# Two weight pieces split on TensorE and ScalarE, and the first layer of two chunks in two halves: one fused attention and MLP kernel with every step in a new order

## The chip, the cores and the metric

The kernel runs on one core of one Trainium2 chip. Its time is the device time of one execution in microseconds (us). Three runs of the kernel before gave 561.91 to 562.13, median 562.1.

## The reference

Inputs are q, k and v of 4 batches, 8 heads, 768 positions and 64 columns, and the weights w_in (512 x 2048) and w_out (2048 x 512), which arrive as 64-bit floats. Cut to what matters:

```
k_sum = k.reshape(B, H, nb, 32, D).max(axis=3)       # one summary key per block of 32
v_sum = v.reshape(B, H, nb, 32, D).mean(axis=3)
scores_l = where(|i - j| < 16, scale * q @ k.T, -1e9)   # a band around the diagonal
scores_s = scale * q @ k_sum.T + log(32)
a = exp(s - max(s));  a = a / (sum(a) + 1e-9)         # s: band and summaries side by side
x = a @ concat(v, v_sum)                               # heads put together: 3072 x 512
h = x @ w_in
out = 0.5 * h * (1 + erf(h / sqrt(2))) @ w_out
```

## The kernel before

The attention is cut into 24 **units**, each one batch, four heads and 256 queries. Two units give the 512 columns of 256 tokens, a **chunk**; there are 12. In a unit of the first batches the steps are: `f_mask`/`f_scores` or `scores` (products on TensorE), `evac` or `add_mask`, `maximum` (an all-reduce over partitions on GpSimd), `m_shift` (TensorE) or `shift` (VectorE), `exponent` (ScalarE), `f_sums`/`sums` and `f_values`/`values` (TensorE), then `norm_take`, `norm_rec`, `norm_spread`, `norm_mult` on VectorE with `norm_cross` on ScalarE between the first two, and last `x_hi` (ScalarE) and `x_lo` (VectorE), which leave the unit's output as a high and a low half in f16.

Nearly all matrix products are three f16 products in place of one f32 product: high by high, high by low, low by high. So each weight is split as well. `w_in` comes in eight **pieces** of 256 columns, one DMA of 1024 KB each (`fetch_w_in`). A piece is turned from the 64-bit pattern into f32 by three VectorE instructions (`wi_bits i 0` to `2`, L458, L463, L467), its high half is written by ScalarE (`wi_hi`, L493) and its low half by one VectorE instruction, `wi_lo` (L496: weight times 128 less the high half). `w_out` goes the same way (`wo_bits`, `wo_hi`, `wo_lo`).

The first layer of chunks 0 to 3 is `phase1 c i` (L990 to L992): 24 products of 128x256, over all four quarters of the contraction, for chunk c and piece i, into one of three PSUM tiles (`psh`). Quarters 0 and 1 come from the chunk's first unit, 2 and 3 from its second. `gelu`, `g_hi` (ScalarE) and `g_lo` (VectorE) follow, and `phase2 c n` (L1109 to L1111) is a quarter of the second layer for half of the tokens. Batches 1 to 3 later take fewer products by Strassen's rule (`sp`, `so` and the sums around them).

Three things matter for the order. All engines work through their instructions strictly in the order in which the program issues them, and a table of steps written out by hand (`ORDER`, some 1,780 steps) sets that order for all engines at once, the DMA issues on SyncE's queue (SP) included. Buffers are handed out by tables of slots (`SLOTS`), so a step also waits until the slot's last user is done. And in the first 36 us the table has steps `fill n`: each is three products of 512 columns or six of 256 of a tile of ones (L409), whose result nobody reads. Sixteen more such products are issued at the start.

Lines that the prediction touches: L409 fill, L618 `sum_vt` (f32 products for the means of v of batch 0), L690 `s_load_vs` (ScalarE copies the means into a unit's v tile), L777 `f_values`, L796 `s_q_hi`, L805 `q_lo`, L949 `norm_cross`, L952 `norm_rec`, L963 `norm_mult`, L970 `x_lo`, L443 `fetch_w_in` and `fetch_w_out`, L666 `load_q`, L675 `load_v`.

Of the kernel before, what the change touches and what calls it, by code (L numbers as in the profile page):

```python
# [79 lines left out]
load_ind, wi_bits 0 0, fetch_k 0 1, f_mask 0, f_scores 0, fetch_vt 0, fill 4, fill 11, load_q 1, evac 0, maximum 0,  # L80
k_pack 2, wi_bits 0 1, wi_bits 0 2, fetch_w_in 4 4, fill 12, sum_vt 0, wi_hi 0, s_k_hi 3, fetch_w_in 5 5, prep_k 0 1,
wi_lo 0, fill 8, k_pack 1, f_mask 1, m_shift 0, load_q 2, m_exponent 0, f_scores 1, f_mask 2, fetch_vt 1, f_sums 0,
fetch_vt 2, evac 1, prep_k_end 0 1, load_v 0, f_scores 2, k_lo 3, load_q 3, wi_bits 4 0, wi_bits 4 1, wi_bits 4 2,
wi_hi 4, wi_bits 5 0, maximum 1, norm_take 0, evac 2, wi_bits 5 1, wi_bits 5 2, norm_cross 0, sum_vt 1, sum_vt 2,
s_q_hi 3, fill 0, mean_vt, m_shift 1, norm_rec 0, s_load_vs 0, fetch_w_in 2 2, load_v 1, f_values 0, fill 3,
norm_spread 0, fetch_w_in 3 3, wi_lo 4, q_lo 3, load_v 2, wi_bits 2 0, m_exponent 1, k_sums 0 1, wi_bits 2 1,
norm_mult 0, maximum 2, s_load_vs 1, x_hi 0, f_sums 1, load_q 4, load_vs 2, m_shift 2, m_exponent 2, wi_bits 2 2,
norm_take 1, x_lo 0, wi_bits 3 0, f_values 1, wi_bits 3 1, load_k 4, f_mask 3, norm_cross 1, scores 3, evac 3,
norm_rec 1, fetch_w_in 1 1, norm_spread 1, load_v 4, wi_hi 5, wi_bits 3 2, fill 10, s_k_hi 4, f_sums 2, norm_mult 1,
x_hi 1, s_q_hi 4, norm_take 2, k_lo 4, wi_hi 3, x_lo 1, maximum 3, load_k 5, wi_lo 5, fill 2, wi_bits 1 0, f_mask 4,  # L90
norm_cross 2, f_values 2, load_v 3, phase1 0 4, fetch_k 1 3, gelu 0 4, q_lo 4, phase1 0 0, wi_bits 1 1, phase1 0 5,
shift 3, wi_hi 2, load_vs 3, wi_bits 1 2, norm_rec 2, load_vs 4, scores 4, exponent 3, norm_spread 2, wi_lo 3, wi_hi
1, g_hi 0 4, fetch_w_in 6 2, norm_mult 2, prep_k 1 3, f_sums 3, wi_lo 2, gelu 0 0, norm_take 3, load_q 5, x_hi 2,
norm_cross 3, f_values 3, wi_lo 1, wi_bits 6 0, gelu 0 5, norm_rec 3, x_lo 2, fetch_k 1 0, fetch_w_in 7 3, norm_spread
3, prep_k 1 0, evac 4, g_hi 0 5, maximum 4, norm_mult 3, phase1 0 3, s_k_hi 5, phase1 0 1, x_hi 3, fetch_w_out 0 4,
g_hi 0 0, wi_bits 6 1, phase1 0 2, s_q_hi 5, k_lo 5, gelu 0 3, fetch_w_out 1 5, x_lo 3, phase1 1 4, q_lo 5, shift 4,
exponent 4, wi_bits 6 2, load_k 6, g_lo 0 4, f_mask 5, gelu 0 1, wo_bits 0 0, s_k_hi 6, f_sums 4, g_lo 0 0, scores 5,
wo_bits 0 1, wi_bits 7 0, load_v 5, g_hi 0 3, g_lo 0 5, f_values 4, gelu 0 2, g_hi 0 1, phase1 1 1, wo_bits 0 2,
fetch_k 2 1, wi_bits 7 1, wo_hi 0, wo_bits 1 0, gelu 1 4, g_lo 0 1, wi_bits 7 2, phase1 1 3, gelu 1 1, fetch_w_out 2
4, norm_take 4, wo_bits 1 1, wo_lo 0, g_lo 0 3, wi_hi 6, wo_bits 1 2, phase1 1 5, wi_hi 7, phase1 1 0, g_hi 1 4, evac  # L100
5, g_lo 1 4, load_q 6, gelu 1 3, wi_lo 7, wo_hi 1, wi_lo 6, f_mask 6, s_q_hi 6, g_hi 0 2, q_lo 6, wo_lo 1, gelu 1 5,
fetch_k 1 1, maximum 5, g_hi 1 5, g_lo 1 5, g_hi 1 1, g_hi 1 3, phase1 1 2, norm_cross 4, phase1 0 7, prep_k 1 1,
prep_k 2 1, wo_bits 2 0, g_lo 1 3, wo_bits 2 1, norm_rec 4, phase2 0 0, wo_bits 2 2, g_lo 0 2, norm_spread 4,
load_mask, gelu 1 2, load_q 7, fetch_w_out 3 5, gelu 1 0, g_hi 1 0, wo_bits 3 0, gelu 0 7, prep_k_end 1 0, wo_bits 3
1, g_lo 1 1, wo_bits 3 2, phase1 0 6, phase1 1 7, k_sums 1 0, k_lo 6, load_vs 5, g_hi 1 2, fetch_w_out 4 4, shift 5,
s_q_hi 7, phase2 0 1, gelu 0 6, norm_mult 4, wo_hi 3, wo_hi 2, exponent 5, wo_lo 3, phase1 1 6, wo_bits 4 0,
fetch_w_out 5 5, wo_lo 2, wo_bits 4 1, scores 6, f_sums 5, evac 6, wo_bits 5 0, wo_bits 4 2, x_hi 4, wo_bits 5 1,
f_values 5, wo_hi 4, norm_take 5, norm_cross 5, wo_bits 5 2, wo_lo 4, f_mask 7, wo_hi 5, load_k 7, wo_lo 5, norm_rec
# [1343 lines left out]
```

## Time and profile before

| | |
|---|---|
| median of three runs | 562.1 us |
| profiled execution | 562.31 us |
| its span, first to last instruction | 560.5 us |
| TensorE busy | 552.6 us, 99% |
| VectorE busy | 472.6 us, 84% |
| ScalarE busy | 384.8 us, 69% |
| GpSimd busy | 94.7 us, 17% |
| DMA | 64.30 MB, mean 115 GB/s |
| granted TensorE clock | 1.000 |

The profiled execution has 1.8 us outside its span and lies 0.2 us above the median. The shares are means over the whole span. VectorE is busy without a break for the first 120 us and has idle time later, and the DMA engines are full from 9 to 30 us only, so what an edit in the first part is worth has to be read from that part.

### The profile page before, as it was taken

What the parts mean: (1) busy time and instruction counts of PE and PEld (TensorE: products, weight loads), DVE (VectorE), ACT (ScalarE), POOL (GpSimd) and SP (SyncE); (2) the same over time, 40 slices, a digit from 0 to 9 for tenths busy, and PEclk for the clock granted to TensorE, in tenths of its full rate; (3) what the DMA queues carried; (4) which work ended last, traced back from release to release, by engine and by line L of the source; (5) the groups of instructions that cost most, each with busy time, mean ns of one, the idle gap of its engine ahead of it and who ended that gap; (6) DMA issues with size and microseconds to landing.
All of it is one profiled execution on the core that took longest, in us unless ns stands there. A gap on an engine that the chain in (4) does not pass through costs nothing.

```text
span 560.5 us, 13994 instructions
## 1 busy us (share of the span) xinstructions
PE 552.6 (99%) x6011; PEld 402.2 (72%) x6011; DVE 472.6 (84%) x660; ACT 384.8 (69%) x665; POOL 94.7 (17%) x42
## 2 busy tenths in 40 slices
...
GB/s 320 396 274 389 189 154 191 266 130 207 158 163 116 146 64 107 144 81 139 91 148 90 28 130 115 63 65 2 22 19 1 20 1 2 2 1 48 1 48 57
DMA packets 29230, 64.30 MB, mean 115 GB/s; under 512 B 2800, under 2 KB 8688, under 8 KB 29168
## 3 DMA queue, kind: packets, MB, share of 16 engines
...
q10 hardware_dynamic: 288, 0.34, 0.2%
q14 instruction: 15, 0.12, 0.1%
HBM read 55.34 MB, written 6.29 MB: 110 GB/s over the span
## 4 chain that ended last, share of the span: by engine, by line
PE 76%; DVE 17%; DMA 3%; issue 2%; ACT 1%; SPq 0%; DVEq 0%
PE psy L1061 13%; PE pso L1109 9%; PE pso L1110 9%; PE pso L1111 9%; PE psz L1061 7%; PE psd_y L1297 4%; PE pso_y L1297 3%; PE pss_x L1297 3%; PE psx L1061 3%; PE psv L913 3%; PE psh L990 2%; PE psh L991 2%; PE psh L992 2%; PE pss L831 2%; DMA w_out_h<-in_vt_dram 2%
## 5 line engine op out<-in xcount | busy, mean ns | idle before, releaser
L860 POOL PARTITION_ALL_REDUCE m<-s x23 | 82.4, 3582 | 284.4 <-DVE s L851 114.2
L1109 PE MATMUL pso<-w_out_h,gg 128*128 128x512 f16 x256 | 97.1, 379 | 0.0
L1111 PE MATMUL pso<-w_out_h,gg 128*128 128x512 f16 x256 | 97.0, 379 | 0.0
L1110 PE MATMUL pso<-w_out_l,gg 128*128 128x512 f16 x256 | 97.0, 379 | 0.0
L1061 PEld LDWEIGHTS <-wt 128*128 128x128 f16 x768 | 74.7, 98 | 12.1 <-issue 0.6
L991 PE MATMUL psh<-xos,ww 128*128 128x256 f16 x256 | 69.8, 273 | 0.8 <-DVE xos L970 0.8
L990 PE MATMUL psh<-xos,ww 128*128 128x256 f16 x256 | 69.8, 273 | 0.1
L1061 PE MATMUL psy<-xos,wt 128*128 128x256 f16 x576 | 69.8, 273 | 0.0
L992 PE MATMUL psh<-xos,ww 128*128 128x256 f16 x256 | 69.8, 273 | 0.0
L1061 PEld LDWEIGHTS <-ww 128*128 128x128 f16 x576 | 56.0, 98 | 9.8 <-issue 0.2
L1111 PEld LDWEIGHTS <-gg 128*128 128x128 f16 x256 | 25.0, 98 | 30.5 <-DVE gg L1093 0.4
L1109 PEld LDWEIGHTS <-gg 128*128 128x128 f16 x256 | 25.0, 98 | 25.9
L1110 PEld LDWEIGHTS <-gg 128*128 128x128 f16 x256 | 25.0, 98 | 25.8
L1297 PEld LDWEIGHTS <-gg 128*128 128x128 f16 x384 | 37.6, 98 | 5.1 <-issue 0.3
L1072 ACT ACTIVATE ww<-psy 128x512 f32<-128x512 f32 x48 | 27.8, 588 | 13.7 <-PE psy L1061 10.9
L1189 DVE SCALAR_TENSOR_TENSOR gg<-h,gg 128x512 f16<-128x512 f32 x32 | 21.7, 684 | 11.1 <-ACT gg L1186 11.1
L1093 DVE SCALAR_TENSOR_TENSOR gg<-g,gg 128x512 f16<-128x512 f32 x32 | 22.7, 711 | 8.0 <-ACT gg L1089 7.9
L865 DVE TENSOR_TENSOR s<-s,m 128x1024 f32<-128x1024 f32 x21 | 25.5, 1217 | 4.3 <-POOL m L860 4.3
L990 PEld LDWEIGHTS <-ww 128*128 128x128 f16 x256 | 25.0, 98 | 4.2 <-issue 0.2
L992 PEld LDWEIGHTS <-ww 128*128 128x128 f16 x256 | 25.0, 98 | 4.1 <-issue 1.2
L991 PEld LDWEIGHTS <-ww 128*128 128x128 f16 x256 | 25.0, 98 | 3.8
L999 ACT ACTIVATE g<-psh 128x512 f32<-128x512 f32 x32 | 18.9, 593 | 11.4 <-DVE gg L1008 8.7
...
## 6 DMA issues: line engine op xcount, KB each, us to landing
...
```

What stands on the lines that cost most here:

```text
L860: nc.gpsimd.partition_all_reduce(out_ap=self.m32, in_ap=self.s32, channels=P, reduce_op=bass_isa.ReduceOp.max)
L865: nc.vector.tensor_tensor(out=self.s32, in0=self.s32, in1=self.m32, op=ALU.subtract)
L990: nc.tensor.matmul(ph[:, e, :], wh, xh, start=(k == 0), stop=False)
L991: nc.tensor.matmul(ph[:, e, :], wh, xl, start=False, stop=False)
L992: nc.tensor.matmul(ph[:, e, :], wl, xh, start=False, stop=(k == NCC - 1))
L1061: nc.tensor.matmul(ps[:, e, :], ws, xx, start=(first and e == 0 and k == 0 and m == 0), stop=(k == 1 and m == 2), skip_group_check=True,)
L1072: nc.scalar.activation(snaps[b, q, n], split8(acc[b, q, "y"]), AF.Copy)
L1093: nc.vector.scalar_tensor_tensor(out=g_part(o // 2, q, 1, fs), in0=g32t.pop((b, q, o)), scalar=SC_G, in1=g_part(o // 2, q, 0, fs), op0=ALU ...
L1109: nc.tensor.matmul(p, gh, w_out_h[:, f, :], start=(f == 0), stop=False)
L1110: nc.tensor.matmul(p, gh, w_out_l[:, f, :], start=False, stop=False)
L1111: nc.tensor.matmul(p, gl, w_out_h[:, f, :], start=False, stop=(f == NFC - 1))
L1297: nc.tensor.matmul(ps, g, ww_, start=(first and e == 0 and k == 0), stop=(e == 1 and k == 2), skip_group_check=True,)
```

## The change

Pieces 0 and 4 of `w_in` get their low halves in another way. `wi_lo 0` and `wi_lo 4` go. In their place TensorE forms 128 times the weight less its high half in PSUM, in two halves of 512 columns (`wi_diff i h`: one f32 product with a scaled identity, one f16 product with a negated one), and ScalarE copies each half to its place (`wi_dlo i h`). `load_neg` makes the negated identity on ScalarE once. `phase1` of chunks 0 and 1 is replaced by `p1h c i 0` and `p1h c i 1`, twelve products each: the first needs only the chunk's first unit and quarters 0 and 1 of the weight. Seven of the nine `fill` steps go. All steps stand in a new order, and the slots follow it.

```
-PE_DIFF = 0
+PE_DIFF = 2
...
 ORDER = '''
-a_load_q 0, fill 1, fetch_k 0 0, prep_k 0 0, a_load_m16, prep_k_end 0 0, k_pack 0, fetch_w_in 0 0, k_sums 0 0,
...
+a_load_q 0, a_load_m16, fetch_k 0 0, prep_k 0 0, k_pack 0, fill 8, prep_k_end 0 0, fetch_w_in 0 0, fetch_vt 0, k_pack
...
+    def p1h(c, i, h):
+        if h == 0:
+            pht[c, i] = ps_h.tile([P, 2, CH], F32, tag="psh", name=f"psh_{c}_{i}")
+        ph, x = pht[c, i], xo[2 * c + h]
+        for e in range(2):
+            for k in range(2):
+                wh, wl = (ww[:, z, 2 * h + k, e, i, :] for z in range(2))
+                xh, xl = (x[:, z, k, :] for z in range(2))
+                for m, (ws, xx) in enumerate(((wh, xh), (wh, xl), (wl, xh))):
+                    nc.tensor.matmul(
+                        ph[:, e, :], ws, xx, start=(h == 0 and e == 0 and k == 0 and m == 0),
+                        stop=(h == 1 and k == 1 and m == 2), skip_group_check=True,
+                    )
```

The steps that are now called and were there unused before:

```
    def load_neg():
        nc.scalar.activation(neg, eye, AF.Copy, scale=-1.0 / SC_WI)
    def wi_diff(i, h):
        ps = diffs["i", i, h] = ps_h.tile([P, 2, CH], F32, tag="psh", name=f"psw_{i}_{h}")
        flat = ps.rearrange("p e j -> p (e j)")
        ks = slice(2 * h, 2 * h + 2)
        nc.tensor.matmul(flat, eye, wt[:, i, h * 512 : (h + 1) * 512], start=True, stop=False)
        nc.tensor.matmul(flat, neg, w_part(i, 0, ks), start=False, stop=True)
    def wi_dlo(i, h):
        flat = diffs.pop(("i", i, h)).rearrange("p e j -> p (e j)")
        ks = slice(2 * h, 2 * h + 2)
        nc.scalar.activation(w_part(i, 1, ks), flat.rearrange("p (r j) -> p r j", j=P), AF.Copy)
```

First place: TensorE around the first `sum_vt` (`psv_vt`). Before:

```order
L409 MATMUL pso_fill_189<-ones 64x512
L618 MATMUL psv_vt<-w_out_h,w_out_l 88x512 x2
L409 LDWEIGHTS ones
L409 MATMUL psd_fill_201<-ones 64x256
L409 LDWEIGHTS ones
L409 MATMUL psd_fill_201<-ones 64x256
```

And after, where `psw` is the PSUM tile of a `wi_diff` and the identities stand in the room of `w_out_l`:

```order
L410 MATMUL psd_fill_178<-ones 64x256
L619 MATMUL psv_vt<-w_out_h,w_out_l 88x512 x2
L505 MATMUL psw_0_196<-wt,w_out_l 128x512
L506 LDWEIGHTS w_out_l
L506 MATMUL psw_0_196<-ww,w_out_l 128x512
L505 MATMUL psw_1_200<-wt,w_out_l 128x512
L506 LDWEIGHTS w_out_l
L506 MATMUL psw_1_200<-ww,w_out_l 128x512
L732 LDWEIGHTS mask_sb
```

The fill behind `sum_vt` has become the two halves of piece 0's low half.

Second place: VectorE from the reciprocal of unit 0 (`rc`) to its `norm_mult` (`x32s<-psv`). Before:

```order
L952 RECIPROCAL rc_287<-rc_287 128x16
L956 STREAM_TRANSPOSE dent_282<-rc_287 128x512
L496 SCALAR_TENSOR_TENSOR ww<-wt,ww 128x1024
L805 TENSOR_TENSOR ql_341<-q_3_273,qh_297 128x512
L458 TENSOR_SCALAR wt<-gg 128x1024
L463 SCALAR_TENSOR_TENSOR wt<-gg,wt 128x1024
L963 TENSOR_TENSOR x32s<-psv_314,dent_282 128x512
L467 SCALAR_TENSOR_TENSOR wt<-gg,wt 128x1024
```

After:

```order
L953 RECIPROCAL rc_284<-rc_284 128x16
L957 STREAM_TRANSPOSE dent_261<-rc_284 128x512
L459 TENSOR_SCALAR wt<-gg 128x1024
L464 SCALAR_TENSOR_TENSOR wt<-gg,wt 128x1024
L468 SCALAR_TENSOR_TENSOR wt<-gg,wt 128x1024
L964 TENSOR_TENSOR x32s<-psv_308,dent_261 128x512
L806 TENSOR_TENSOR ql_343<-q_3_255,qh_326 128x512
```

The low half of piece 4 is gone, the third step of piece 2 has moved ahead of `norm_mult`, and the low half of unit 3's q has moved behind it.

Third place: DMA issues on SP from `load_q 2` on. Before, where `gg` is the raw room for pieces 2 and 3:

```order
L666 DMA q_2_219<-in_qd_dram 128x512
L612 DMA w_out_h<-in_vt_dram 128x1024 x2
L675 DMA v_0_254<-in_vw_dram 128x1024
L666 DMA q_3_273<-in_qd_dram 128x512
L443 DMA gg<-in_w_in_dram 128x4x512
L675 DMA v_1_312<-in_vw_dram 128x1024
```

After:

```order
L667 DMA q_2_185<-in_qd_dram 128x512
L613 DMA w_out_h<-in_vt_dram 128x1024 x2
L444 DMA gg<-in_w_in_dram 128x4x512
L676 DMA v_0_223<-in_vw_dram 128x1024
L667 DMA q_3_255<-in_qd_dram 128x512
L444 DMA gg<-in_w_in_dram 128x4x512
L676 DMA v_1_328<-in_vw_dram 128x1024
```

Piece 2 (1024 KB) now goes ahead of unit 0's v (512 KB) and unit 3's q (256 KB).

## Rows read from the trace of the kernel before

**Rows 1.** The page: busy time, share of the span, instructions.

```profile
PE 552.6 (99%) x6011; PEld 402.2 (72%) x6011; DVE 472.6 (84%) x660; ACT 384.8 (69%) x665; POOL 94.7 (17%) x42
```

**Rows 2.** Waits of TensorE: who, for whom; us, times, longest.

```profile
PE psn L785 <- ACT s L868: 1.0, 1, 1.0
PE pso_fill_s L409 <- POOL warm L421: 0.9, 1, 0.9
PE psh L991 <- DVE xos L970: 0.8, 2, 0.5
PE psv L777 <- issue: 0.6, 1, 0.6
```

**Rows 3.** Busy us by stretch: PE, PEld, DVE, ACT, POOL; clock, DMA, GB/s.

```profile
10.00:20.00 10.00, 9.66 (x84) 5.53 (x82) 9.86 (x11) 6.58 (x11) 3.84 (x1) 1.00 1.05 398
20.00:30.00 10.00, 9.67 (x100) 5.61 (x96) 9.76 (x11) 7.59 (x16) 7.32 (x2) 1.00 1.04 391
...
100.00:120.00 20.00, 19.54 (x150) 14.37 (x148) 19.67 (x27) 14.92 (x24) 4.19 (x1) 1.00 0.57 205
...
200.00:300.00 100.00, 100.00 (x1148) 66.90 (x1141) 92.49 (x134) 77.36 (x132) 17.99 (x6) 1.00 0.35 106
```

**Rows 4.** Waits of VectorE, 0 to 120 us: all of them.

```profile
DVE ks_f L591 <- DMA w_out_l<-in_kp_dram: 6.2, 1, 6.2
DVE wt L458 <- DMA gg<-in_w_in_dram: 0.8, 1, 0.8
```

**Rows 5.** Timeline of TensorE: start, duration, line, operation, count, [idle before].

```profile
0.94 5.61 PE L409 MATMUL pso_fill_s<-ones 128*64 128x512 f16 x16 [0.94 <-POOL warm L421]
...
10.43 0.83 PE L409 MATMUL pso_fill<-ones 128*64 128x512 f16 x3
11.10 0.82 PE L409 MATMUL psd_fill<-ones 128*64 128x256 f16 x6
...
12.91 1.92 PE L618 MATMUL psv_vt<-w_out_h,w_out_l 128*88 128x512 f32 x4 [0.34 <-DMA w_out_h<-in_vt_dram]
...
27.66 1.15 PE L777 MATMUL psv<-s,v 128*64 128x64 f32 x32
...
39.55 0.27 PE L991 MATMUL psh<-xos,ww 128*128 128x256 f16 x1 [0.37 <-DVE xos L970]
...
46.53 0.27 PE L992 MATMUL psh<-xos,ww 128*128 128x256 f16 x1
...
107.98 0.27 PE L991 MATMUL psh<-xos,ww 128*128 128x256 f16 x1 [0.46 <-DVE xos L970]
```

**Rows 6.** Timeline of VectorE, the same columns.

```profile
14.00 1.25 DVE L496 SCALAR_TENSOR_TENSOR ww<-wt,ww 128x1024 f16<-128x1024 f32 x1
...
25.21 2.00 DVE L496 SCALAR_TENSOR_TENSOR ww<-wt,ww 128x1024 f16<-128x1024 f32 x1
27.14 0.68 DVE L805 TENSOR_TENSOR ql<-q,qh 128x512 f16<-128x512 f32 x1
...
29.83 0.68 DVE L963 TENSOR_TENSOR x32s<-psv,dent 128x512 f32<-128x512 f32 x1
30.43 1.22 DVE L467 SCALAR_TENSOR_TENSOR wt<-gg,wt 128x1024 int32<-128x1024 int32 x1
...
37.53 1.36 DVE L799 TENSOR_TENSOR k_all<-k,k_all 128x640 f16<-128x640 f32 x1
...
89.53 0.82 DVE L799 TENSOR_TENSOR k_all<-k,k_all 128x640 f16<-128x640 f32 x1
...
107.23 0.69 DVE L970 TENSOR_TENSOR xos<-x32s,xos 128x512 f16<-128x512 f32 x1
```

**Rows 7.** Timeline of ScalarE, the same columns.

```profile
25.28 0.63 ACT L796 ACTIVATE qh<-q 128x512 f16<-128x512 f32 x1 [1.19 <-DMA q<-in_qd_dram]
...
26.55 1.05 ACT L690 ACTIVATE v<-w_out_h 24x1024 f32<-24x1024 f32 x1
...
41.60 0.60 ACT L999 ACTIVATE g<-psh 128x512 f32<-128x512 f32 x1
```

More of the change, by code (lines that the diff above doesn't have):

```diff
@@ L78 @@
 ORDER = '''
-a_load_q 0, fill 1, fetch_k 0 0, prep_k 0 0, a_load_m16, prep_k_end 0 0, k_pack 0, fetch_w_in 0 0, k_sums 0 0,
[L80 to L108, printed above, removed]
@@ new lines @@
+wi_dlo 0 1, load_q 3, wi_hi 4, k_sums 0 0, wi_bits 5 1, norm_take 0, wi_bits 5 2, f_mask 2, f_scores 2, evac 2,
+norm_cross 0, sum_vt 1, sum_vt 2, k_sums 0 1, norm_rec 0, norm_spread 0, maximum 2, fetch_w_in 3 3, wi_diff 4 0,
+m_shift 1, mean_vt, s_load_vs 0, f_values 0, wi_bits 2 0, s_q_hi 3, load_v 1, m_shift 2, load_v 2, wi_dlo 4 0, load_vs
+2, fetch_k 1 3, wi_bits 2 1, wi_bits 2 2, norm_mult 0, m_exponent 1, q_lo 3, wi_bits 3 0, f_sums 1, fetch_w_in 1 1,
+wi_diff 4 1, norm_take 1, x_hi 0, m_exponent 2, norm_cross 1, x_lo 0, f_mask 3, load_q 4, load_k 4, wi_bits 3 1,
@@ new lines @@
+s_load_vs 1, scores 3, evac 3, norm_rec 1, norm_spread 1, wi_bits 3 2, f_sums 2, f_values 1, norm_mult 1, prep_k 1 3,
+load_v 4, p1h 0 4 0, wi_hi 5, x_hi 1, wi_dlo 4 1, p1h 0 0 0, x_lo 1, p1h 0 4 1, maximum 3, f_values 2, wi_lo 5, wi_hi
+3, p1h 0 0 1, shift 3, norm_take 2, p1h 0 5 0, s_q_hi 4, exponent 3, s_k_hi 4, f_sums 3, q_lo 4, wi_lo 3, k_lo 4,
+norm_cross 2, fetch_w_out 0 4, wi_bits 1 0, wo_bits 0 0, norm_rec 2, wi_bits 1 1, p1h 0 5 1, gelu 0 0, norm_spread 2,
+load_v 3, g_hi 0 0, p1h 0 3 0, gelu 0 5, load_q 5, f_mask 4, s_q_hi 5, scores 4, wi_bits 1 2, wi_hi 2, fetch_k 1 0,
```

332 lines of the change are left out of this document (176 added, 156 removed).

## The prediction

> **What bounds the kernel now.** I read the page first. TensorE is busy for 552.6 of 560.5 us [rows 1], so in all 7.9 us can be won on it, unless its work shrinks. The waits come next: TensorE lists 3.3 us in its four largest entries [rows 2]; about 3 us more lie behind its last product, where results are stored. Then the table by stretch: from 200 to 300 us TensorE has no idle time at all, and from 10 to 30 us some 0.3 us in each 10 [rows 3]. But in that first part "busy" is no measure of use, since fill products, which nobody reads, count too. So the next view is the other engine: VectorE is 98 to 99% busy between 10 and 30 us and between 100 and 120 [rows 3], and after 9.2 us it waits for nothing up to 120 us; the two waits listed end before that [rows 4]. It is the engine that paces the beginning. The last place where TensorE visibly waits for it is the product at 107.98 us [rows 5], which needs the low half of unit 5, written by VectorE from 107.23 to 107.92 [rows 6]. From there to the end TensorE runs nearly without a gap. So the time is: the moment at which that low half is there, plus a fixed amount of TensorE work, plus the store. The question is how much earlier `x_lo 5` comes, and whether something else takes its place.
>
> **TensorE's own sum.** Seven fills go. One costs 0.67 us, the distance of two starts, 10.43 and 11.10 [rows 5]: 4.7 us less. Four `wi_diff` come. None is in the trace; its two products are like others there. Two f32 products of 512 columns took 1.92 us in `sum_vt` (four records) [rows 5], so one is 0.96; one f16 product of 512 columns is a third of a fill, 0.22. That is 1.2 us each, 4.7 for four. From below, if the f32 product with a 128-column identity went at f16 speed, it would be 0.44 each, 1.8 in all, and 2.9 us would be won; from above, if its weights were loaded unhidden at half a product more, 1.7 each and 2 us lost. I take 4.7, since `sum_vt` has the same moving shape: the sum is nil. Splitting `phase1` costs nothing in products: 24 become 12 and 12, at 0.109 us each (39.55 to 46.53, 64 steps) [rows 5]. It lets the first layer start after one unit.
>
> **VectorE's sum.** `wi_lo 0` (1.25 us) and `wi_lo 4` go. The second took 2.00 us, and the next instruction started 1.93 later [rows 6]; GpSimd was busy for 7.32 of those 10 us [rows 3], and I put the excess over 1.25 down to that. So 2.5 us of work goes, 3.2 as measured. Up to `x_lo 5` the rest is the same but for one instruction of half a tile's width swapped for another. If VectorE stayed as full as it was, `x_lo 5` would come 2.5 to 3.2 us earlier.
>
> **What that saving meets.** It does not stay full. The reciprocal of unit 0 hangs on `norm_cross 0`, and that on ScalarE, which now has `wi_dlo 0 1` and the copies of the summaries ahead of it; a `wi_dlo` has no row, and the nearest, an ACTIVATE from PSUM of the same 128x512, took 0.60 [rows 7] (below, nothing; above, 1.05, the 1024-wide one [rows 7]). So the reciprocal comes no earlier than before, and the first `wi_lo` only turns into idle time. Next, the DMA order: piece 2 now goes ahead of unit 0's v. In the kernel before, unit 3's q had landed at 25.28, when `s_q_hi 3` stopped waiting for it [rows 7]; up to and with that q 7,928 KB had been asked for (sizes by the tiles' shapes, 1024 KB for a piece of w_in, 512 for v). In the changed kernel 8,696 KB stand up to and with unit 0's v, 768 KB more, which at 391 GB/s [rows 3] are 2.0 us: v lands at about 27.3. Behind it come `s_load_vs 0` (1.05) [rows 7], `f_values 0` (1.15) [rows 5], and so `norm_mult 0` starts at 29.6, against 29.83 before [rows 6]: 0.2 us earlier. By then VectorE has done the third step of piece 2 (1.22) in advance [rows 6] and still owes the low half of q (0.68) [rows 6]. Its lead in useful work is 1.22 - 0.68 + 0.2 = 0.7 us, and the remainder of the 2.5 is idle. Ends: if v is there in time, `f_values 0` is bound by TensorE's own queue, where `wi_diff 4 0` stands ahead of it, and the lead is 1.3; for each us that v comes later, one us is lost.
>
> From there to `x_lo 1` the chains are alike, but in the kernel before the low half of unit 4's k fell beside GpSimd and took 1.36 instead of 0.82 us [rows 6]; it has moved behind `x_lo 1`. That may add 0.5. Against it, the shift of unit 3 stands earlier on VectorE and may wait a few tenths for the maximum on GpSimd. I take a lead of 1.0 us at `x_lo 5`, 106.9 instead of 107.92, and so 1.0 off the end. TensorE itself is early enough: it can do two half tiles, 24 products or 2.6 us, before `x_lo 1` is there, where before it had to stop at the eighth product, at 39.55 [rows 5]. So it reaches `x_lo 5` some 2 us too soon, and an error of that size in the price of `wi_diff` does not move the end.
>
> **A second gate.** The new order asks for the last low half of w_out (`wo_lo 7`) sooner. Behind `x_lo 5` VectorE has 16 steps up to it: eight of 1024 columns at 1.2, six of 512 at 0.6 (29.83 to 30.43 [rows 6]) and 1.2 for the summaries of k, 14.4 us. TensorE has five tiles less seven products (12.3) and the first seven products of the second layer's last quarter (1.5), 13.8. So this gate opens at the same time as the first, or half a us later. It takes nothing from the forecast as long as no instruction there is stretched.
>
> **ScalarE** gains four `wi_dlo` and `load_neg`, about 2.7 us, in a stretch where it is 66 to 76% busy [rows 3]; I charge it only where named above. **The end**: the last product is again one of the final second-layer group, with one copy and one store behind it. Nothing changes there.
>
> **The clock.** The fills also keep TensorE active. The granted clock is 1.00 in every stretch of the table [rows 3], which is the 2.4 GHz level; only the sixteen products at the start, from idle, took 5.61 us, 0.35 each against 0.22 later [rows 5], so they began at the 1.2 GHz level. The Trainium skill, "TensorE: Matmul & The Clock Gate", section "What's actually happening", says that the throttled state is the default and activity lifts it. By that rule a kernel with seven fills fewer could fall back; the trace agrees about the start and shows no fall after it. In place of the fills stand real products, so I hold a fall for unlikely. It would double the time of the products for as long as it lasts, up to 0.22 us for each of 512 columns, several us before the first layer starts.
>
> **The sum.** The profiled execution took 562.31, with 560.5 of span. 560.5 - 1.0 + 1.8 = 561.3, and as it lies 0.2 above the median, the forecast is 561.1 us. A measurement of this kernel can tell about 0.2%, 1.1 us, from no change; the forecast lies at that edge.
>
> **Rivals.**
> *Full gain.* The early waits of VectorE do not come (v in time, `wi_lo 4`'s stretched 1.93 us vanish for good), and `x_lo 5` is 2.5 to 3.2 us earlier. For it: VectorE's gapless 110 us. Against: the DMA order. Then TensorE's own waits limit the gain, at about 2.5: 559.6. Chance 0.17.
> *Nothing.* The lead is eaten on the way, at `wo_lo 7` or the shift of unit 3: one VectorE instruction stretched as at 25.21 (0.7 us more than its like) is enough. 562.0 give or take 0.5. Chance 0.18.
> *Slower.* Piece 2 delays unit 0's v by more than the bytes say. For it: in the trace `s_q_hi 3` waited 1.19 us for a small request [rows 7]. Against: the rate is an even 391 to 398 GB/s [rows 3]. The gain is gone if v lands 1.0 us later than 27.3, and past 29.4 the kernel is slower by more than can be told apart; the whole chain `norm_mult 0`, `x_lo 0` to `x_lo 5` moves with it. At 30 us: 562.1 + 1.7 = 563.8. Chance 0.12.
> *The clock falls*, as above: 565 or more. Chance 0.03.
>
> **Chances.** The forecast, 560.2 to 562.0, has 0.50. Its own half below 561.0 gives 0.27 to faster and 0.23 to no change. With the full gain, faster by over 0.2% is 0.44; with "nothing" mostly inside, no change is 0.38; slower is 0.18 (0.12, 0.03 and 0.03 of the third case's edge). The range takes in most of the full gain and the nearer part of the slower one: 559.3 to 562.9.
>
> **What would show it.** Right: `norm_mult 0` starts at 29 to 30 us with idle time of VectorE before it, put down to TensorE or a DMA; `norm_rec 0` waits for ScalarE; `x_lo 5` ends near 106.9; TensorE waits about 1 to 2 us in all for VectorE between 60 and 125 us, more than the 0.5 at 107.98; each `wi_diff` takes 1.2 us and each `wi_dlo` 0.6. Wrong: VectorE without idle time from 10 to 30 us (then the full gain), v of unit 0 landing behind 28.5, a granted clock under 1.00 after 10 us, or new waits of TensorE behind 125 us, where there were almost none. A new wait there, in the 430 us whose order was changed as well, would be the part that I have no row for.

## The result, and the profile after

The changed kernel took 565.23 us (median of 4 runs, 564.13 to 565.41) against 562.03 of the kernel before (4 runs, 561.91 to 562.13): ratio 1.0051, interval 1.0039 to 1.0063. It is 3.2 us slower; the forecast was 561.1, and the range ended at 562.9. Its profiled execution took 565.41 with a span of 563.5.

The page's row on busy time, and TensorE's waits (engine, line, for whom; us, times, longest), to be read against [rows 1, 2]:

```profile
PE 553.6 (98%) x5996; PEld 401.9 (71%) x5996; DVE 468.8 (83%) x658; ACT 391.0 (69%) x672; POOL 94.4 (17%) x42
```

```profile
PE pss L764 <- ACT kf L751: 1.1, 1, 1.1
PE psh L1004 <- ACT g L1014: 1.1, 2, 0.8
PE psh L1004 <- DVE ww L497: 1.0, 1, 1.0
...
PE psv L914 <- DVE x32s L964: 0.8, 1, 0.8
PE psh L991 <- ACT g L1014: 0.4, 1, 0.4
PE psv L778 <- issue: 0.4, 1, 0.4
PE pss L832 <- DVE s L852: 0.3, 1, 0.3
```

TensorE is 1.0 us busier and 2.0 us idler. Where, the table by stretch shows: busy us of PE, PEld, VectorE, ScalarE, GpSimd, then granted clock, DMA share, GB/s. First the kernel before, then the changed one:

```profile
0.00:40.00 40.00, 36.76 (x371) 20.88 (x372) 32.35 (x38) 25.73 (x47) 18.55 (x19) 1.00 0.92 338
40.00:60.00 20.00, 20.00 (x250) 17.44 (x248) 19.97 (x26) 17.48 (x26) 6.90 (x3) 1.00 0.93 336
60.00:110.00 50.00, 48.43 (x502) 35.12 (x499) 49.67 (x62) 34.36 (x57) 9.49 (x3) 1.00 0.58 206
110.00:210.00 100.00, 100.00 (x1265) 68.29 (x1264) 96.64 (x131) 82.13 (x134) 24.56 (x7) 1.00 0.48 138
```

```profile
0.00:40.00 40.00, 37.79 (x352) 21.83 (x353) 29.45 (x36) 26.73 (x47) 16.80 (x19) 0.96 0.95 352
40.00:60.00 20.00, 18.62 (x256) 15.79 (x253) 19.90 (x26) 15.54 (x30) 6.53 (x3) 1.00 0.81 291
60.00:110.00 50.00, 48.21 (x495) 34.25 (x493) 49.83 (x61) 34.48 (x54) 9.46 (x3) 1.00 0.57 202
110.00:210.00 100.00, 98.49 (x1263) 68.45 (x1262) 92.45 (x128) 80.55 (x134) 23.66 (x6) 1.00 0.51 150
```

Behind 40 us the changed kernel's TensorE idles 1.38, 1.79 and 1.51 us where the one before idled 0, 1.57 and 0: 3.1 us more, the whole difference of the spans. At 40 us both have the same work ahead: span less 40, less the idle time (before 0.1 more behind 210 us) and a tail of 3.0 behind the last product, is 515.8 for both. So TensorE has no lead at 40 us, and then there is a loss.

The page's chain, followed back from the last instruction, shows by its shares what the end hangs on. First the kernel before, then the changed one:

```profile
PE 76%; DVE 17%; DMA 3%; issue 2%; ACT 1%; SPq 0%; DVEq 0%
```

```profile
PE 68%; DVE 1%; issue 0%; ACT 0%; DVEq 0%
```

Before, it runs over TensorE back to 107.98 us and from there over VectorE, as the prediction took it. In the changed kernel it leaves TensorE at 178.02 us already, for `norm_mult 8` on VectorE, and it is lost at 172.8; no product there is seen to wait for `x_lo 5`.

The waits of TensorE and the VectorE rows that go with them (start, duration, line, operation, count, [idle before]), in the changed kernel:

```profile
53.66 0.61 PE L1004 MATMUL psh<-xos,ww 128*128 128x256 f16 x4 [1.00 <-DVE ww L497]
...
66.62 1.58 PE L1004 MATMUL psh<-xos,ww 128*128 128x256 f16 x13 [0.78 <-ACT g L1014]
...
178.02 0.22 PE L914 MATMUL psv<-ph,vh 128*64 128x64 f16 x2 [0.76 <-DVE x32s L964]
```

```profile
25.11 0.25 DVE L953 RECIPROCAL rc<-rc 128x16 f32<-128x16 f32 x1 [2.99 <-ACT rc L950]
...
26.04 1.60 DVE L459 TENSOR_SCALAR wt<-gg 128x1024 int32<-128x1024 int32 x1
...
30.10 0.68 DVE L964 TENSOR_TENSOR x32s<-psv,dent 128x512 f32<-128x512 f32 x1
...
37.44 0.92 DVE L971 TENSOR_TENSOR xos<-x32s,xos 128x512 f16<-128x512 f32 x1
...
50.69 2.91 DVE L497 SCALAR_TENSOR_TENSOR ww<-wt,ww 128x1024 f16<-128x1024 f32 x1
...
57.67 0.69 DVE L971 TENSOR_TENSOR xos<-x32s,xos 128x512 f16<-128x512 f32 x1
...
108.02 0.68 DVE L971 TENSOR_TENSOR xos<-x32s,xos 128x512 f16<-128x512 f32 x1
...
135.07 1.23 DVE L866 TENSOR_TENSOR s<-s,m 128x1024 f32<-128x1024 f32 x1 [3.12 <-POOL m L861]
```

```profile
50.51 3.35 POOL L861 PARTITION_ALL_REDUCE m<-s  x1 [1.75 <-ACT rc L945]
```

Three things are to be seen. VectorE idles 2.99 us ahead of `norm_rec 0`. `wi_lo 1` at 50.69 takes 2.91 us, beside the all-reduce of `maximum 4` that began at 50.51; its like takes 1.21. And by its end, `x_lo 1` (37.44) is 1.1 us earlier than before, `x_lo 3` (57.67) 1.0 later and `x_lo 5` (108.02) 0.8 later [rows 6]. The two rows of the kernel before that were not shown:

```profile
38.81 0.68 DVE L970 TENSOR_TENSOR xos<-x32s,xos 128x512 f16<-128x512 f32 x1
...
56.71 0.68 DVE L970 TENSOR_TENSOR xos<-x32s,xos 128x512 f16<-128x512 f32 x1
```

### The profile page after: what moved, and what is told of

It reads as the page before. It is cut to its first block, busy times and chain, and to the rows that moved or that the text cites. A ratio compares the mean times of both kernels' runs of the same rounds, so it can differ in the third digit from the quotient of the medians.

```text
span 563.5 us, 13950 instructions
## 1 busy us (share of the span) xinstructions
PE 553.6 (98%) x5996; PEld 401.9 (71%) x5996; DVE 468.8 (83%) x658; ACT 391.0 (69%) x672; POOL 94.4 (17%) x42
## 4 chain that ended last, share of the span: by engine, by line
PE 68%; DVE 1%; issue 0%; ACT 0%; DVEq 0%
PE psy L1076 15%; PE psz L1076 7%; PE pso L1124 7%; PE pso L1126 7%; PE pso L1125 7%; PE psx L1076 4%; PE psd_y L1312 4%; PE pso_y L1312 4%; PE pss_x L1312 4%; PE psv L914 2%; PE pss L832 2%; PE psv_z L1312 2%; PE psn L930 1%; PE psh L991 1%; PE psh L993 1%; PE psh L992 1%
## 5 line engine op out<-in xcount | busy, mean ns | idle before, releaser
L861 POOL PARTITION_ALL_REDUCE m<-s x23 | 83.9, 3650 | 284.5 <-DVE s L852 112.8
L1076 PEld LDWEIGHTS <-ww 128*128 128x128 f16 x576 | 56.0, 98 | 9.0 <-issue 0.2
L1004 PE MATMUL psh<-xos,ww 128*128 128x256 f16 x384 | 43.9, 273 | 2.1 <-ACT g L1014 1.1
L1004 PEld LDWEIGHTS <-ww 128*128 128x128 f16 x384 | 37.0, 98 | 8.6 <-issue 2.3
L991 PE MATMUL psh<-xos,ww 128*128 128x256 f16 x128 | 34.9, 273 | 0.4 <-ACT g L1014 0.4
L866 DVE TENSOR_TENSOR s<-s,m 128x1024 f32<-128x1024 f32 x21 | 27.1, 1291 | 9.6 <-POOL m L861 9.6
L993 PE MATMUL psh<-xos,ww 128*128 128x256 f16 x128 | 34.9, 273 | 0.0
L992 PE MATMUL psh<-xos,ww 128*128 128x256 f16 x128 | 34.9, 273 | 0.0
L869 ACT ACTIVATE s<-s 128x1024 f32<-128x1024 f32 x21 | 22.2, 1057 | 8.0 <-DVE s L866 7.8
L881 DVE TENSOR_TENSOR pl<-s,ph 128x1024 f16<-128x1024 f32 x18 | 22.1, 1230 | 3.0 <-ACT ph L877 3.0
```

Source lines behind the costliest of these rows:

```text
L861: nc.gpsimd.partition_all_reduce(out_ap=self.m32, in_ap=self.s32, channels=P, reduce_op=bass_isa.ReduceOp.max)
L866: nc.vector.tensor_tensor(out=self.s32, in0=self.s32, in1=self.m32, op=ALU.subtract)
L991: nc.tensor.matmul(ph[:, e, :], wh, xh, start=(k == 0), stop=False)
L992: nc.tensor.matmul(ph[:, e, :], wh, xl, start=False, stop=False)
L993: nc.tensor.matmul(ph[:, e, :], wl, xh, start=False, stop=(k == NCC - 1))
L1004: nc.tensor.matmul(ph[:, e, :], ws, xx, start=(h == 0 and e == 0 and k == 0 and m == 0), stop=(h == 1 and k == 1 and m == 2), skip_group_c ...
```

## The experiments

All are timed in five rounds beside the kernel before (medians of 562.06 to 562.34 in the four groups). One measure orders them: the end of `x_lo 3`, and what is left of the span from there ("rest").

| kernel | median us | ratio, 95% | x_lo 3 ends | span | rest |
|---|---|---|---|---|---|
| before | 562.03 | | 57.39 | 560.5 | 503.1 |
| changed | 565.23 | 1.0051 (1.0039 to 1.0063) | 58.36 | 563.5 | 505.1 |
| e1_fill | 564.36 | 1.0034 (1.0021 to 1.0047) | 58.21 | 563.3 | 505.1 |
| e2_shift_later | 567.36 | 1.0085 (1.0071 to 1.0098) | 58.71 | 566.0 | 507.3 |
| e3_new_order_old_halves | 567.49 | 1.0086 (1.0073 to 1.0099) | 60.22 | 565.8 | 505.6 |
| e4_old_order_new_halves | 564.48 | 1.0038 (1.0026 to 1.0050) | 59.85 | 563.0 | 503.1 |
| e5_max4_later | 565.63 | 1.0060 (1.0047 to 1.0073) | 57.81 | 563.1 | 505.3 |
| e6_old_sbuf_beside_max4 | 564.42 | 1.0041 (1.0028 to 1.0055) | 58.70 | 562.6 | 503.9 |
| e7_norm_beside_max | 565.50 | 1.0065 (1.0052 to 1.0078) | 58.10 | 563.0 | 504.9 |
| e8_together | 566.63 | 1.0079 (1.0066 to 1.0091) | 59.51 | 565.8 | 506.3 |
| e9_two_waits | 564.93 | 1.0046 (1.0034 to 1.0058) | 58.28 | 563.4 | 505.1 |
| h1_new_then_old | 563.96 | 1.0029 (1.0018 to 1.0040) | 57.65 | 561.4 | 503.8 |
| h2_old_then_new | 564.26 | 1.0042 (1.0027 to 1.0057) | 57.06 | 561.3 | 504.2 |
| h3_mended_then_old | 563.73 | 1.0025 (1.0014 to 1.0035) | 58.17 | 561.9 | 503.7 |
| e10_v_first | 565.89 | 1.0058 (1.0045 to 1.0070) | 58.94 | 564.1 | 505.2 |
| e11_shift4_early | 564.99 | 1.0048 (1.0036 to 1.0061) | 58.29 | 563.5 | 505.2 |
| e12_mended_then_old | 565.04 | 1.0049 (1.0035 to 1.0062) | 59.89 | 564.4 | 504.5 |
| e13_old_order_halves | 562.73 | 1.0006 (0.9997 to 1.0015) | 57.03 | 560.2 | 503.2 |

The last three columns are of the profiled execution alone. The runs of one kernel with the new order lie up to 3.6 us apart, so a profiled span can lie off its median; the profiled executions of e5, e7, h1, h2 and e13 were their fastest, those of the changed kernel, e1, e3, e4, e8, e11 and e12 their slowest.

### First group: the clock, the shifts, and each half of the change alone

**e1_fill** gives TensorE work where it stood idle ahead of the clock's fall.

```
- f_mask 0, fetch_k 0 1,
+ f_mask 0, fill 1, fetch_k 0 1,
```

> The changed kernel with one more fill of three products behind f_mask 0, where TensorE stood idle for 1.11 us before its granted clock fell to 0.83 (10 to 20 us). Theory A (the orders of VectorE and GpSimd set the time, TensorE's early part is not the gate): the clock stays at 1.00 there, TensorE waits longer for VectorE later, and the time is that of the changed kernel within 0.4 us, 565.2. Rival B (the clock fall sets it): the 1.85 us that the slow products took come back, 563.4. If the clock falls in spite of the fill, this run tells nothing of B.

Granted clock 10 to 20 us: 0.83 in the changed kernel, 1.00 here. The rows, the changed kernel first:

```profile
10.00:20.00 10.00, 10.00 (x66) 5.43 (x68) 9.43 (x11) 5.50 (x9) 3.33 (x1) 0.83 1.04 397
```

```profile
10.00:20.00 10.00, 10.00 (x88) 5.93 (x84) 9.43 (x11) 6.29 (x10) 3.22 (x1) 1.00 1.04 397
```

TensorE does 22 instructions more there, and `x_lo 1` ends 0.8 us earlier (37.59); at `x_lo 3` 0.15 is left of it. The median is 0.9 lower than the changed kernel's, but the intervals overlap and the two were timed in different groups. Neither theory is met exactly. Two runs of the changed kernel with a mean clock of 1.000 had spans of 563.5 and 563.4, so the fall is not what made it slow.

**e2_shift_later** moves work into VectorE's two idle stretches of 3.12 us.

```
+ prep_k_end 2 0, q_lo 9, norm_rec 6, norm_spread 6, prep_v 2 1,
  shift 7, v_hi 6, v_lo 6
...
+ norm_cross 8 (ahead of v_hi 9)
+ g_lo 2 5, norm_rec 8, norm_spread 8, norm_mult 8, v_lo 9,
  shift 11
```

> The changed kernel with five VectorE steps moved ahead of shift 7 and five ahead of shift 11 (with norm_cross 8 ahead of v_hi 9 on ScalarE), so that VectorE no longer stands idle 3.12 us twice for GpSimd's maximum. Theory A (a shift too close behind its maximum is what is late behind 125 us): TensorE's waits of 0.32, 0.30 and 0.76 us between 140 and 180 us go, and with them 0.8 to 1.5 us: 563.7 to 564.4. Rival B (all was lost before 125 us, or these waits are replaced by others): within 0.4 us of 565.2. Rival C (the shifted exponents are then late): slower than 565.2.

Slower than the changed kernel by 2.1 us: rival C. The shift behind the first stretch started at 137.47 us and not at 135.07. VectorE, from this kernel:

```profile
132.03 1.97 DVE L800 TENSOR_TENSOR k_all<-k,k_all 128x640 f16<-128x640 f32 x1 [0.46 <-ACT k_all L740]
...
145.99 2.01 DVE L806 TENSOR_TENSOR ql<-q,qh 128x512 f16<-128x512 f32 x1 [0.58 <-ACT qh L797]
```

`k_lo` takes 1.97 instead of 0.81, `q_lo` 2.01 instead of 0.68; the all-reduces began at 130.79 and 145.56. TensorE then waits 1.52 at 148.05 for that `ql`. Neither row is of a step that the list moved. Unit 9's `k_lo` started 0.70 us behind its all-reduce in the changed kernel too, and took 0.81 there; it is 1.24 behind here. Unit 8's `q_lo` began just ahead of its all-reduce there, and here just behind it. So a step's time hangs on where it meets an all-reduce, and that gave theory D of the next group.

**e3_new_order_old_halves** and **e4_old_order_new_halves** take the change apart: the new order without the TensorE part, and the TensorE part in the old order.

```
e3: - wi_diff 0 0, wi_dlo 0 0, wi_diff 0 1 ... wi_dlo 4 1, load_neg
    + fill 4, wi_lo 0, fill 12 ... wi_lo 4 (ahead of norm_rec 0), fill 1, fill 10
e4: - wi_lo 0, wi_lo 4, fill 12, fill 8, fill 3, fill 10
    + load_neg, wi_diff 0 0, wi_dlo 0 0, wi_diff 0 1, wi_dlo 0 1,
      wi_diff 4 0, wi_dlo 4 0, wi_diff 4 1, wi_dlo 4 1
```

> The changed kernel with the first two low halves of w_in on VectorE again (wi_lo 0 in place of wi_dlo 0 0, wi_lo 4 in the idle time ahead of norm_rec 0), and a fill in place of each of the four wi_diff. The new order and the halves of the first layer stay. Theory A (the new order costs the time, the TensorE part gives little): 565.2 give or take 0.7, above the kernel before (562.0) by about as much as the changed kernel. Rival B (the TensorE part is what costs, by the clock, by ScalarE or by f32 products): near 562.0. Rival C (the TensorE part brings its 2.5 us and the order loses more): 566.5 or more.

> The kernel before, with the same four wi_diff and wi_dlo in place of wi_lo 0 and wi_lo 4, load_neg behind evac 0, and four fills less; its order is otherwise kept, and the first layer is not halved. Theory A (the part does what it says, and the new order takes it back): x_lo 5 comes 1 to 2.5 us earlier than 107.92 and the time is 559.8 to 561.3. Rival B (VectorE's saving turns into idle time in any order): 562.0 give or take 0.4. Rival C (ScalarE or the clock pays for it): 563 or more, with a granted clock under 1.00 between 10 and 30 us or VectorE waiting for ScalarE.

e3 is 2.3 us slower than the changed kernel (rival C): in the new order the TensorE part is worth that. VectorE was full from 13 us on, and two steps fell beside the all-reduces of units 1 and 2, which began at 19.41 and 23.18:

```profile
19.63 2.38 DVE L458 TENSOR_SCALAR wt<-x32s 128x1024 int32<-128x1024 int32 x1
...
23.56 2.66 DVE L467 SCALAR_TENSOR_TENSOR wt<-x32s,wt 128x1024 int32<-128x1024 int32 x1
```

e4 is 2.1 us slower than the kernel before (nearest to rival C, though the clock stayed at 1.00), and all of it lies ahead of `x_lo 3`; its rest is that of the kernel before. VectorE waited for TensorE's sums of unit 0, which came later behind the new products, and TensorE, at a `wi_diff`, for its slot:

```profile
21.41 0.45 DVE L936 STREAM_TRANSPOSE dent<-psn 128x256 f32<-128x256 f32 x1 [1.15 <-PE psn L785]
```

```profile
32.20 1.12 PE L504 MATMUL psw<-wt,w_out_l 128*128 128x512 f32 x2 [0.58 <-ACT ww L510]
```

So e4 shows that this placement in the old order loses, not that every one would.

### Second group: the neighbours of the all-reduce

```
e5: evac 4: from ahead of norm_take 3 to behind g_hi 0 4 (maximum 4 starts later)
e6 (kernel before): wi_bits 6 1: from behind norm_mult 3 to ahead of prep_k 1 0
e7: norm_rec 6, norm_spread 6, prep_v 2 1 ahead of shift 7;
    norm_rec 8, norm_spread 8, norm_mult 8 ahead of shift 11; norm_cross 8 ahead of v_hi 9
e8: e1 + e5 + e7, and wo_bits 0 0 behind wi_bits 1 2
```

> The changed kernel with one step of ScalarE moved: evac 4 behind g_hi 0 4, so that GpSimd's maximum 4 starts at about 52.1 us instead of 50.51, behind wi_lo 1 and not beside it. Theory D (a VectorE instruction that reads and writes only SBUF is held while the first 1.8 us of an all-reduce run, so its neighbours decide the time): wi_lo 1 falls from 2.91 to about 1.21 us, TensorE's wait of 1.00 at 53.66 goes, x_lo 5 ends 1.4 to 1.7 us earlier than 108.70, and the time is 563.5 to 564.0. Rival B (this wait is not the gate, or the loss moves to the next instruction beside the all-reduce): within 0.4 us of 565.2.

> The kernel before with one step of VectorE moved: wi_bits 6 1 (integer, SBUF to SBUF) ahead of prep_k 1 0 and norm_mult 3, so that it starts 0.1 us behind the start of maximum 4 at 53.08 and not 1.51. No work is added. Theory D: it takes 2.7 to 3.0 us instead of 1.46, x_lo 5 ends 1.2 to 1.6 us later than 107.92, and the time is 563.2 to 563.9. Rival B (VectorE's order beside an all-reduce does not matter, or 1.4 us there are caught up): 562.3 give or take 0.4.

> The changed kernel with only steps that are not held by an all-reduce (reciprocal, transpose, product from PSUM, a reduction) moved into the 3.12 us in which VectorE waits for maximum 7 and 11: norm_rec 6, norm_spread 6 and prep_v 2 1 ahead of shift 7; norm_rec 8, norm_spread 8 and norm_mult 8 ahead of shift 11, with norm_cross 8 ahead of v_hi 9 on ScalarE. Theory D: these run at their usual times, TensorE's wait of 0.76 at 178.02 for norm_mult 8 goes, and the time is 563.9 to 564.6. Rival B (the loss behind 125 us comes back elsewhere, as when the held steps were put there: then 0.80 at 195 and 0.78 at 202): 565.2 or more.

> The changed kernel with the fill behind f_mask 0, evac 4 behind g_hi 0 4, wo_bits 0 0 behind wi_bits 1 2 (VectorE waited 0.53 for its DMA when the fill alone was put in), and the moves ahead of shift 7 and 11. Theory D: the gains add up, 0.8 (measured for the fill) + 1.5 + 0.5 + 0.7 = 3.5, so 561.7, and x_lo 5 near 106.5: the changed kernel then is no slower than the one before, and what was wrong was the order beside the all-reduces. Rival B (some other limit of the new order lies under these): 563 or more.

**e6** is the simplest test: one step of the kernel before is moved, no work added. Its VectorE, GpSimd, and TensorE with the stretch behind its wait:

```profile
52.97 2.89 DVE L463 SCALAR_TENSOR_TENSOR wt<-gg,wt 128x1024 int32<-128x1024 int32 x1
...
56.64 0.67 DVE L963 TENSOR_TENSOR x32s<-psv,dent 128x512 f32<-128x512 f32 x1
```

```profile
52.89 3.22 POOL L860 PARTITION_ALL_REDUCE m<-s  x1 [4.93 <-ACT s L847]
```

```profile
59.55 0.27 PE L990 MATMUL psh<-xos,ww 128*128 128x256 f16 x1 [2.52 <-ACT g L999]
```

```profile
60.00:65.00 5.00, 5.00 (x38) 3.29 (x37) 5.00 (x7) 4.16 (x5) 0.00 (x0) 0.66 0.56 200
```

2.89 us instead of 1.46, `x_lo 3` 1.3 later, `x_lo 5` 1.8 later (109.72), the time 2.4 later: the hold is as theory D has it, and the cost larger. Not all of the cost is the hold. The step now also stands ahead of `norm_mult 3`, which starts at 56.64 and not at 53.99: about 1.2 us of that is the step's own time, the rest the hold. ScalarE waits for `norm_mult 3`, and TensorE 2.52 us at 59.55 for ScalarE. Behind that wait the granted clock fell, 0.66 from 60 to 65 us. The fall is not what made e6 slow: two of its executions with a mean clock of 1.000 had spans of 563.0 and 562.5.

**e5** gives `wi_lo 1` its 1.21 us back, but another step falls beside the moved all-reduce (52.78):

```profile
50.38 1.21 DVE L497 SCALAR_TENSOR_TENSOR ww<-wt,ww 128x1024 f16<-128x1024 f32 x1
...
53.66 1.56 DVE L971 TENSOR_TENSOR xos<-x32s,xos 128x512 f16<-128x512 f32 x1 [0.49 <-ACT xos L968]
```

`x_lo 2` takes 1.56 instead of 0.64. `x_lo 3` comes 0.55 earlier, and the median shows nothing: rival B, though by the means theory D describes.

**e7** removes the wait at 178 us, but 0.80 and 0.78 us come back at 192.58 and 199.65 (`q_lo` at 182.99 was held, 2.11 us): no gain. **e8** is worse than each of its parts; there VectorE waited for the DMAs too, and `f_values 3` 1.69 us at 50.18.

### Third group: the two orders joined

e9 moves three steps of the changed kernel. In e9 and h3 `norm_mult 3` writes its buffer ahead of `x_lo 2`, so the low half of unit 2 is computed from unit 3's values there; nothing is left out. h1 is the changed kernel up to and with `x_lo 5`, then the remaining steps in the old order; h2 the kernel before up to and with `x_lo 3`, then the new order; h3 is h1 with e9's moves and e1's fill.

```
e9: evac 4 behind g_hi 0 4; norm_mult 3 ahead of x_lo 2; exponent 4 behind g_hi 0 1
```

> The changed kernel with three steps moved: evac 4 behind g_hi 0 4 (the all-reduce no longer beside wi_lo 1), norm_mult 3 ahead of x_lo 2 (the product from PSUM is not held, x_lo 2 was when evac 4 alone was moved: 1.56 us), and exponent 4 behind g_hi 0 1 (ScalarE stood 1.51 us for shift 4 at 63.61, with two tables loaded around it and gelu 0 1 behind it, when TensorE waited 0.78 at 66.62 for a psh slot). Theory F (behind 40 us TensorE paces in both kernels; the loss is the sum of its waits, 4.55 us behind 40 against 1.6 before): the waits of 1.00 and 0.78 go, 565.2 - 1.8 = 563.4, 563.0 to 564.2. Rival B (each wait removed comes back at the next gate, as for evac 4 alone, where 0.40 and 0.39 came back): 564.6 or more.

> The changed kernel up to and with x_lo 5 (108.70 us), and from there the steps that are left in the order of the kernel before (buffers given out anew, the longest free first). Theory G (the order behind 125 us costs 1.4 to 2.2 us by itself: from the end of x_lo 5 to the end of the span it is 454.8 us in the changed kernel, 452.6 in the one before): TensorE has no waits between 140 and 200, and the time is 562.8 to 563.6. Rival B (what is left of TensorE's work at x_lo 5 is more in the new order's first part, and the rest only shows it): 564.6 to 565.6.

> The kernel before up to and with x_lo 3 (57.4 us), so without the TensorE part and without halves of the first layer in what is done by then, and from there the steps that are left in the order of the changed kernel. Theory G: the waits between 140 and 180 us (1.4 in all) and the one at 66 us (0.8) are there again, and the time is 563.5 to 564.8 though the early part is that of the kernel before. Rival B (the loss is made in the first 57 us): 561.9 to 562.6.

> The changed kernel's first part with the three steps of e9_two_waits moved and one fill behind f_mask 0, then from x_lo 5 on the order of the kernel before. Theories F and G together: 565.2 - 1.8 - 1.8 - 0.4 = 561.2, 560.6 to 561.8: faster than the changed kernel by 4 us and than the one before by 0.5 to 1.5. If only one of them holds: 562.8 to 563.6.

In **e9** both waits went, and 1.13 us came back at 69.12 for a `psh` slot: rival B. **h1** and **h2** split the loss. Their stretch from 110 to 210 us, h1 first:

```profile
110.00:210.00 100.00, 100.00 (x1268) 68.50 (x1266) 96.26 (x130) 81.20 (x133) 23.69 (x7) 1.00 0.49 144
```

```profile
110.00:210.00 100.00, 99.25 (x1268) 68.86 (x1267) 94.83 (x128) 81.64 (x135) 23.75 (x7) 1.00 0.50 150
```

With the old order from `x_lo 5` on, TensorE waits for nothing there, and the median falls by 1.3 us (0.4 above theory G's range, well under rival B's); the profiled execution agrees, with a rest of 503.8 against 505.1. So most of the loss behind `x_lo 3` goes with the late order. Order and buffers are not separated: h1 also hands out its buffers anew from there on. And its first part, whose program is the changed kernel's, went otherwise in the profiled execution: VectorE waited 1.35 us for ScalarE at 49.31, and `wi_lo 1`, at 51.39, was not held. So which steps meet an all-reduce can differ between executions of one order. With the old order up to `x_lo 3`, `x_lo 3` is as early as in the kernel before, and the median is still 2.1 above it, within theory G's range; of the waits that it named, 0.64 at 67.11 came again, and 0.42 and 0.33 between 140 and 180 us in place of 1.4 in all. **h3** gained nothing that h1 did not have.

### Fourth group: what eats VectorE's saving, and who paces the kernel before

```
e10: fetch_w_in 2 2 behind load_v 0
e11: maximum 4, shift 4 behind x_lo 3
e12: e10 + e11 + e5 + e1, from wo_bits 6 0 on in the old order
e13 (kernel before): - fill 2, phase1 0 4, phase1 0 0
                     + p1h 0 4 0 (in its place), p1h 0 0 0, p1h 0 4 1, p1h 0 0 1
```

> The changed kernel with one DMA moved: piece 2 of w_in (fetch_w_in 2 2) behind unit 0's v (load_v 0), as in the kernel before. Theory H (the DMA order eats VectorE's saving: 1024 KB ahead of v are 2.6 us at 391 GB/s): norm_mult 0 starts 0.8 us or more ahead of 30.10, TensorE has 0.5 to 1.0 us less work left at 40 us than 515.8, and the time is 564.2 to 564.8. Rival B (v is not what is late; piece 2 is then late in its place): work left at 40 us within 0.3 of 515.8, time 565.2 give or take 0.4.

> The changed kernel with maximum 4 and shift 4 moved behind x_lo 3 in the list, so that VectorE shifts unit 4 at about 58 us and not 62.4, and ScalarE, which stood 1.51 us for it at 63.61, drains gelu 0 1 earlier. Theory F: TensorE's wait of 0.78 at 66.62 goes or falls under 0.2 and the time is 564.2 to 564.8. Rival B (three psh slots are too few for the order of the halves, whatever ScalarE does): a wait of 0.5 or more between 60 and 72 us is still there, and 565.2 give or take 0.4.

> The changed kernel's first part with v ahead of piece 2, the fill behind f_mask 0, evac 4 behind g_hi 0 4 and shift 4 early, and from wo_bits 6 0 on (109 us) the order of the kernel before. If the parts add up: 565.2 - 0.7 - 0.4 - 0.5 - 0.7 - 1.3 (the late part, as measured with the old order from x_lo 5 on) = 561.6, 561.0 to 562.4: no slower than the kernel before. If waits removed come back at the next gate, as they did so far: 563 or more.

> The kernel before with the first two first-layer tiles (0 4 and 0 0) in halves: p1h 0 4 0 in place of fill 2, p1h 0 0 0 ahead of p1h 0 4 1, so that TensorE has 1.3 us more real work ahead of x_lo 1 in place of a fill. VectorE's order is untouched. Theory J (behind 40 us TensorE paces in the kernel before too): 0.7 to 1.0 us earlier, 561.1 to 561.6. Rival (VectorE paces until x_lo 5, as the forecast took it): x_lo 5 ends within 0.3 us of 107.92, TensorE waits some 1 us more for it at 108 us, and the time is 562.2 give or take 0.3.

**e10**: theory H falls. `norm_rec 0` does not wait, which is not the move's doing: in e5, with the DMA order of the changed kernel, it started at 23.42 without a wait as well. Piece 2 is late in v's place, 2.83 us against 1.41 in e5:

```profile
23.52 0.25 DVE L953 RECIPROCAL rc<-rc 128x16 f32<-128x16 f32 x1
...
27.36 0.69 DVE L459 TENSOR_SCALAR wt<-gg 128x1024 int32<-128x1024 int32 x1 [2.83 <-DMA gg<-in_w_in_dram]
```

**e11**: the wait at 66 us went, 0.50 came back at 61.91 and 0.20 at 74.65: rival B. **e12** fell too; `f_values 3` waited 2.06 us at 50.31 and VectorE 1.61 for a piece of w_out at 45.70.

**e13** settles the first step of the forecast. By the sum made above TensorE has 513.8 us of work left at 40 us, 2.0 less than in the kernel before. Of these 1.6 are lost at one place, `f_values 3`:

```profile
47.59 0.59 PE L776 MATMUL psv<-s,v 128*64 128x64 f32 x13 [1.61 <-issue]
```

```profile
46.81 0.68 DVE L962 TENSOR_TENSOR x32s<-psv,dent 128x512 f32<-128x512 f32 x1
...
106.89 0.69 DVE L969 TENSOR_TENSOR xos<-x32s,xos 128x512 f16<-128x512 f32 x1
```

`norm_mult 2`, which frees the only `psv` tile, ended at 47.49, and 0.1 later TensorE went on. The time did not change (ratio 1.0006, 0.9997 to 1.0015): VectorE paces the kernel before up to there, the rival of that run, though not by its numbers (the wait came at 47.59 and not at 108, and 562.73 is 0.2 above its range), and halves of the first layer alone bring nothing. None of these 16 kernels beats the one before.

## Why the prediction was wrong, step by step

**That VectorE sets a gate and the rest is a fixed amount.** Half right. In both orders the span is the end of `x_lo 3` plus a rest that the early part touches little: 503.1 to 503.2 in the kernel before, e4 and e13 (503.9 in e6); 505.1 to 505.3 in the changed kernel, e1, e5, e9, e10 and e11 (505.6 in e3). `x_lo 5` comes a fixed time behind `x_lo 3` (50.5 us from end to end before, 50.3 after); the prediction had it end at 106.9, and it ended at 108.70. The step that failed above all is the fixed amount: the new order's rest is 2.0 us longer. Of these, 1.6 are waits of TensorE behind `x_lo 3`, and 0.4 is work that it had put off by then. And `x_lo 5` is no longer the gate, as the chain shows. This is the larger part of the miss, two thirds of the 3.0 us. The prediction said of a wait behind 125 us that it had no row for it, and put no case on it; such waits came, 1.38 us in all at 146 and 178. h1 places about 1.3 us of it behind `x_lo 5`.

**TensorE's own sum.** Right in its terms. Two `wi_diff` halves start 1.08 us apart (14.39 and 15.47), 4.3 for four against 4.7 expected, and seven fills less 4.7. What was held unlikely came as well, for a moment:

```profile
8.26 2.00 PE L764 MATMUL pss<-q,kf 64*128 64x64 f32 x32 [1.11 <-ACT kf L751]
10.19 1.16 PE L410 MATMUL psd_fill<-ones 128*64 128x256 f16 x6
11.28 3.28 PE L619 MATMUL psv_vt<-w_out_h,w_out_l 128*88 128x512 f32 x4
14.39 1.02 PE L505 MATMUL psw<-wt,w_out_l 128*128 128x512 f32 x2
```

Behind 1.11 us without work, the fill took 1.16 instead of 0.82 and the four records of `sum_vt` 3.28 instead of 1.92 [rows 5]; the granted clock of 10 to 20 us was 0.83, so part of it was granted at 1.2 GHz and not 2.4. By the Trainium skill, "TensorE: Matmul & The Clock Gate", section "What's actually happening", activity is what lifts the clock from its default. The trace agrees in that the fall came behind idle time; but TensorE stood idle for 1.93 us at 33.59 in e3 and for 2.06 at 50.31 in e12, and no fall followed. The fall is not what made the kernel slow, as e1 and the runs at 1.000 show. So it is chance that the rival "the clock falls", with its fall and its 565 or more, is the one that fits the measured numbers.

**The saving and its early waits.** The size was right. The steps that VectorE has done by `x_lo 3` come to 2.4 us less than before at their usual durations: 5.1 us that were done by then and are not now (the two `wi_lo`, `k_lo 5`, `wi_bits 6 0` and `6 1`), 2.7 the other way. Idle time rose by 3.0 us, nearly all of it the 2.99 ahead of `norm_rec 0`, where ScalarE was named as the cause. When that wait is short or absent, as in e1, e5 and e10, the last step of piece 5 is held beside `maximum 1` (20.80 in e5, 2.55 us instead of 1.23) and VectorE stands for piece 2 of w_in. From `norm_rec 0` to `norm_mult 0` VectorE ran without a gap in the changed kernel, so the landing of v, the largest term of that sum, set nothing there. `norm_mult 0` started at 30.10, not 29.6; the clock's fall is in it (29.28 in e1).

**The lead of 1.0 us.** It was there up to `norm_mult 2`: that started 0.6 later than before (47.78 against 47.17), with 1.6 us of other steps done ahead (`prep_k 1 3`, `wo_bits 0 0`). Then `wi_lo 1` met `maximum 4` and took 1.7 us more than its like. The step that failed here is the one from "From there to `x_lo 1` the chains are alike" to a lead of 1.0 us at `x_lo 5`: it looked at what is beside GpSimd at 37 us, and not at which step the new order would put beside the next all-reduce. In e6 such a meeting, with what the move put off besides, cost 2.4 us in the old order. e5 shows that this one can't simply be taken out: the next step is held instead. Holds as such are not new: up to `x_lo 3`, stretched instructions add 3.1 us to VectorE before (1.35 of it at 20.54) and 3.4 after. What changed is where they fall.

**The rivals.** "Nothing" named the mechanism (one stretched VectorE instruction is enough) at 0.7 us; it measured 1.7, and not at either of the two places named. "Slower", by a late v of unit 0, was not it (e10).

**What stays open.** Which steps of the late order make the 1.3 to 2.0 us: e2 and e7 changed two suspected places, and the waits went elsewhere. Whether the buffers, which h1 and h2 hand out anew, have a part in it. And how much of the early loss is the all-reduce alone: each wait that was removed came back in part, 0.4 to 1.6 us, at the next gates.
